# A delta-rule attention block and a gated feed-forward block on one core: two more units fetched in blocks, one more pair's first layer by 20 block products, and a new order of all work

## The chip, the core and the metric

The kernel runs on one core of one Trainium2 chip. The metric is device time in microseconds. Before the change it was measured in three runs: 637.15, 640.19 and 640.47 us, with a median of 640.19.

A core has five engines that run beside each other and wait for one another through semaphores. TensorE (PE in the profile, with PEld for the loads of its stationary operand) does matrix products. VectorE (DVE), ScalarE (ACT) and GpSimd (POOL) do elementwise work. SyncE (SP) starts transfers; ScalarE and GpSimd can start them too. Each engine takes its instructions in the order in which they were written, so an instruction that waits holds up all that stand behind it on its engine.

## What is computed

```python
# 4 batches, 8 heads, 768 positions, head size 48
k_n = k / (norm(k) + 1e-06)
state = zeros(4, 8, 48, 48)
for t in range(768):
    y[:, :, t] = q[:, :, t] @ state
    v_old = state^T @ k_n[:, :, t]
    state += beta[:, :, t] * outer(k_n[:, :, t], v[:, :, t] - v_old)
x = y as (3072 tokens, 384)
h = x @ w_in            # 384 -> 2048
g = h * cos(h)
out = g @ w_out         # 2048 -> 384
```

## The kernel before

**Units and pairs.** The 768 positions are cut into 24 units of 32. The four batches fill the 128 partitions. Within a unit the recurrence is written as a triangular system: the products of all keys with each other (the gram matrix) give a 32 x 32 triangle for each batch and head, whose inverse is needed to get the unit's updates. Only the 48 x 48 states pass from unit to unit. Two units make a pair of 256 tokens; there are 12 pairs, and the feed-forward block runs pair by pair.

**One unit**, in the names of its tasks (function `unit`, L1492): load k, q and v; norms of k (`square`, `sum`, `norms`, `scale`); `turn`, which puts k and q with the head dimension on partitions; `gram` (L673), whose results VectorE scales and masks into g (`gram_keys`, L694) and tt (`gram_queries`, L813); the inverse of the triangle; then the serial part: `state` (L928, products with the state), `right` (L945), `solve` (L1000, or L958, L958, L994 in three steps for units 2 and 3), `solve_out` (L1012), `update` (L1025), `update_out` (L1033), `within` (L1043 or L1055), `within_out` (L1068), `features` (L1076) and `features_out` (L1084). Unit n+1's `state` needs unit n's `update_out`.

**Inverses, three ways.** Units 0 and 1 invert by doubling: six rounds of small products on TensorE (`double`, L757), each followed by copies, additions and 32 x 32 transposes on ScalarE and VectorE. All others go pair by pair, the 16 matrices of a partition group laid out so that GpSimd can eliminate column by column: g is written to DRAM (`gram_put`), read back (`gram_get` into gb), inverted by pairs of operations (`inv`, L877 and L884), written to DRAM (`put`) and read back as zt (`get`). gb, z and zt have one buffer each. Pair 1 (units 2 and 3) does this at half size.

**Two ways of turning.** For units below `PLAIN_TURNS` (8) k and q are loaded whole, TensorE turns them (L640, eight transposes a unit) and ScalarE copies the result out (L650). From `PLAIN_TURNS` on, k and q are fetched a second time in blocks of 32 columns (`load_blocks`, L415, eight transfers a unit), which VectorE turns by 32 x 32 transposes (`turn_blocks`, L660, four a unit); k is loaded in eight parts instead of four and g stored in three instead of one, with half of the heads on swapped partitions ("home"), and `weigh` and beta follow that.

**The feed-forward block.** The first layer is computed two ways. For pairs in `ONES` (0 and 1) it is plain: eight groups (`hidden`, L1097) of twelve products. For the others (`gated`) 20 block products (`layer`, L1271) of sums of x blocks (`x_sum`, L1186) with sums of w_in blocks (`in_sums`, L1233, 22 of them once, twelve in place in w_in, so that they must follow the last plain group) replace the 24 block products of a plain first layer, and the results are put together by copies on ScalarE (L1283, L1285) and additions on VectorE (L1288). Then come x cos x by ScalarE and VectorE (`turns` L1134, `rest` L1141, `cos` L1150, `gate` L1153) and the second layer: plain for pair 0 (`out`, L1295), by seven products of half size (L1353, with sums of gates L1369, sums of w_out L1382 and collecting L1405) for the rest. The weights come as 64-bit words and are narrowed to 32 bits on chip, 28 pieces in the tasks `weights`, `split`, `shift` and `add`; the pieces' buffers are those of the gates.

**The order of the work.** Nothing schedules at run time. Every piece of work is a task with the tasks it depends on and the buffers it makes and uses (`add`); the arguments for cost, transfer time and due time are those of a planner that isn't part of the kernel. `Order.LINE` lists all tasks by number in the order in which they are written out, `Order.OTHER` the tasks that go to the second choice of two engines or queues:

```python
def queue(*key):
    return nc.scalar if key in Order.OTHER else nc.sync
...
        for key in line:
            emit, deps, makes, uses = self.tasks[key]
            assert deps <= done, key
```

Which buffer a task gets follows from the order too. At the end every instruction is pinned behind the one before it on its engine, and transfers behind each other across SP's and ScalarE's queues.

**Unread products.** `keep_warm` (L493) multiplies a constant tile into the output bank, and nobody reads it. `WARM_FIRST` (5) are written at the start; `WARMS` (56) are tasks, each of which does something only as long as no output product has been written (31 of the 56).

Of the kernel before, what the change touches and what calls it, by code (L numbers as in the profile page):

```python
# [59 lines left out]
class Order:  # L60

    OTHER = {
        ('gram_put', 2), ('q', 3), ('gram_get', 1), ('inv', 1, 0), ('put', 1), ('gram_put',
        4), ('gram_put', 5), ('v', 7), ('v', 8), ('v', 9), ('blocks', 11, 1), ('gram_put',
        11), ('put', 5), ('v', 13), ('put', 6), ('gram_put', 15), ('gram_get', 7), ('get',
        15), ('v', 16), ('blocks', 16, 0), ('blocks', 16, 1), ('gram_put', 16), ('blocks',
        18, 1), ('k', 19), ('blocks', 19, 0), ('gram_get', 9), ('get', 19), ('gram_put',
        20), ('v', 21), ('gram_put', 21), ('put', 10), ('gram_put', 22), ('v', 23),
        ('gram_put', 23), ('gram_get', 11), ('right', 4, 4), ('left', 1, 1, 0), ('left', 1,
        3, 0), ('left', 1, 3, 1), ('store', 1, 0), ('x_sum', 2, 'd'), ('x_sum', 2, 'n'),  # L70
        ('x_sum', 2, 'm'), ('x_sum', 2, 'e'), ('x_sum', 2, 'k'), ('x_sum', 2, 'g'),
        ('x_sum', 2, 'i'), ('x_sum', 2, 'l'), ('x_sum', 2, 'f'), ('x_sum', 2, 'b0'),
        ('left', 2, 4, 1), ('left', 2, 3, 1), ('x_sum', 3, 'd'), ('x_sum', 3, 'n'),
        ('x_sum', 3, 'm'), ('x_sum', 3, 'e'), ('x_sum', 3, 'k'), ('x_sum', 3, 'g'),
        ('x_sum', 3, 'i'), ('x_sum', 3, 'l'), ('x_sum', 3, 'h'), ('x_sum', 3, 'b0'),
        ('left', 3, 4, 1), ('left', 3, 3, 1), ('x_sum', 4, 'd'), ('x_sum', 4, 'm'),
        ('x_sum', 4, 'g'), ('x_sum', 4, 'i'), ('left', 4, 3, 0), ('left', 4, 3, 1),
        ('store', 4, 0), ('x_sum', 5, 'd'), ('x_sum', 5, 'e'), ('x_sum', 5, 'l'), ('x_sum',
        5, 'h'), ('x_sum', 5, 'b0'), ('left', 5, 2, 0), ('left', 5, 4, 1), ('left', 5, 3,
        0), ('left', 5, 3, 1), ('store', 5, 0), ('x_sum', 6, 'd'), ('x_sum', 6, 'g'),  # L80
        ('x_sum', 6, 'l'), ('x_sum', 6, 'f'), ('x_sum', 6, 'b0'), ('left', 6, 1, 0),
        ('left', 6, 4, 0), ('store', 6, 1), ('x_sum', 7, 'd'), ('x_sum', 7, 'm'), ('x_sum',
        7, 'g'), ('x_sum', 7, 'i'), ('x_sum', 7, 'f'), ('x_sum', 7, 'h'), ('x_sum', 7,
        'b0'), ('left', 7, 4, 0), ('left', 7, 4, 1), ('left', 7, 3, 1), ('x_sum', 8, 'd'),
        ('x_sum', 8, 'm'), ('x_sum', 8, 'e'), ('x_sum', 8, 'k'), ('x_sum', 8, 'g'),
        ('x_sum', 8, 'l'), ('left', 8, 3, 0), ('store', 8, 0), ('store', 8, 1), ('x_sum', 9,
        'd'), ('x_sum', 9, 'm'), ('x_sum', 9, 'e'), ('x_sum', 9, 'k'), ('x_sum', 9, 'i'),
        ('x_sum', 9, 'l'), ('x_sum', 9, 'b0'), ('left', 9, 1, 0), ('left', 9, 2, 0),
        ('left', 9, 1, 1), ('left', 9, 3, 0), ('store', 9, 0), ('x_sum', 10, 'k'), ('x_sum',
        10, 'i'), ('x_sum', 10, 'l'), ('x_sum', 10, 'h'), ('x_sum', 10, 'b0'), ('left', 10,  # L90
        1, 0), ('left', 10, 1, 1), ('left', 10, 4, 1), ('left', 10, 3, 0), ('left', 10, 3,
        1), ('store', 10, 0), ('x_sum', 11, 'd'), ('x_sum', 11, 'e'), ('x_sum', 11, 'k'),
        ('x_sum', 11, 'g'), ('x_sum', 11, 'f'), ('left', 11, 1, 0), ('left', 11, 2, 0),
        ('left', 11, 1, 1), ('left', 11, 3, 0), ('left', 11, 3, 1), ('store', 11, 1),
        ('store_right', 11), ('weights', 5), ('weights', 7), ('weights', 15), ('weights',
        16), ('weights', 18), ('weights', 20), ('weights', 22), ('weights', 23), ('weights',
        25), ('weights', 27)
    }

    WARM_FIRST, WARMS = 5, 56  # L100
    LINE = """
# [138 lines left out]
def kernel(  # L240
# [1197 lines left out]
    ONES, PLAIN = range(2), range(1)  # L1438
# [508 lines left out]
```

## Time and profile before

The profile is of one execution. Its span, from the first to the last instruction, is 636.6 us; 24189 instructions are in it. The time of a run has what lies around the span in it, and the three runs shown lie 0.5 to 3.9 us above this span.

| engine | busy, us | share of the span |
|---|---|---|
| TensorE products | 619.2 | 97% |
| TensorE weight loads | 576.2 | 90% |
| VectorE | 495.1 | 78% |
| GpSimd | 435.8 | 68% |
| ScalarE | 297.7 | 47% |

How to read it: an engine's busy time is the time in which an instruction of it was under way, a wait for a semaphore not counted. A plain float32 product stands as two records (two passes), a transpose as one. In rows of the timeline the columns are start, duration, engine, line, operation, result<-operands, size, count, and in brackets the idle time before it with what ended it. In rows of the stretches, the busy time of each engine is followed by the count of instructions; then come the clock that was granted to TensorE (1.00 is full), the share of the transfer engines and their rate.

Three waits, from the groups of the page: GpSimd's inversions (L877) stood idle 21.2 us for gb from DRAM, ScalarE's L1150 waited 42.6 us for VectorE, and VectorE's L1405 28.0 us for TensorE's second layer.

### The profile page before, as it was taken

How to read it: one execution, taken by the hardware profiler on the slowest of the kernel's cores; microseconds unless marked ns; L12 is line 12 of the kernel's file. 1: busy time of each engine (PE TensorE's matmuls, PEld its weight loads, DVE VectorE, ACT ScalarE, POOL GpSimd, SP SyncE). 2: the span in 40 equal slices, each digit the busy share in tenths (PEclk: the TensorE clock that was granted, in tenths of full speed). 3: DMA queues.
4: the chain of work that ended last, by engine and by line, in shares of the span. 5: the costliest groups of instructions: out<-in, count | busy, mean ns of one | idle time of the engine just before them, and what ended most of it. 6: DMA issues, size and time to landing. Idle time of an engine off the chain costs nothing.

```text
span 636.6 us, 24189 instructions
## 1 busy us (share of the span) xinstructions
PE 619.2 (97%) x10176; PEld 576.2 (90%) x10176; DVE 495.1 (78%) x1030; ACT 297.7 (47%) x528; POOL 435.8 (68%) x780
## 2 busy tenths in 40 slices
PE   5999989999999999999999999999999999999997
PEld 4877877987899999999999999999999999999997
DVE  5776656779998999887898888888888776566682
ACT  3457556562423444643642644733643553545440
POOL 5247788678788788887789888886884883112241
PEclk8899999999999999999999999999999999999999
DMA  8978656563651555435435344333304102000001
GB/s 173 221 171 213 121 155 146 93 118 60 116 68 22 94 90 99 60 67 104 61 70 98 56 73 90 58 57 67 74 3 81 44 1 43 19 2 26 1 25 26
DMA packets 209381, 50.37 MB, mean 79 GB/s; under 512 B 200920, under 2 KB 204280, under 8 KB 209272
## 3 DMA queue, kind: packets, MB, share of 16 engines
q1 hardware_dynamic: 161896, 35.03, 29.3%
q10 hardware_dynamic: 47072, 13.25, 10.0%
q8 instruction: 80, 1.31, 0.9%
q0 software_dynamic: 304, 0.54, 0.4%
q14 instruction: 29, 0.24, 0.1%
HBM read 38.55 MB, written 10.22 MB: 77 GB/s over the span
## 4 chain that ended last, share of the span: by engine, by line
PE 90%; DVE 3%; DMA 3%; ACT 1%; issue 1%; POOL 0%; SPq 0%; ACTq 0%; DVEq 0%
PE p_out L1353 29%; PE p_h L1271 27%; PE p_h L1097 6%; PE p_kq L928 4%; PE p_out L1295 3%; PE p_s L1025 3%; PE p_g L673 3%; PE p_h L757 3%; PE p_kq L1055 3%; PE p_u L1000 3%; PE p_out L493 2%; PE p_h L1353 2%; PE p_z L1076 1%; DMA kp<-in_k_dram 1%; PE p_t L640 1%
## 5 line engine op out<-in xcount | busy, mean ns | idle before, releaser
L877 POOL TENSOR_TENSOR part<-z,gb 128x126 f32<-128x126 f32 (+23 forms) x321 | 144.6, 451 | 46.7 <-DMA gb<-g_dr 21.2
L884 POOL TENSOR_TENSOR z<-z,part 128x126 f32<-128x126 f32 (+23 forms) x321 | 145.5, 453 | 25.1
L1353 PE MATMUL p_out<-w_out,g_ffn 128*128 128x192 f32 x672 | 121.9, 328 | 0.3 <-DVE o L1405 0.2
L1353 PEld LDWEIGHTS p_out<-w_out,g_ffn 128*128 128x128 f32 x672 | 107.7, 190 | 1.7 <-DVE o L1405 0.7
L1150 ACT ACTIVATE turns<-turns,halfpi 128x512 f32<-128x512 f32 x96 | 68.0, 719 | 55.7 <-DVE turns L1141 42.6
L1353 PE MATMUL p_out<-w_sum,g_ffn 128*128 128x192 f32 x496 | 89.7, 329 | 0.2 <-DVE o L1405 0.2
L1271 PE MATMUL p_h<-x_sum,w_in 128*128 128x128 f32 x640 | 84.0, 277 | 0.0
L1134 ACT ACTIVATE turns<-g_ffn,quarter_turn 128x512 int32<-128x512 f32 x70 | 49.8, 719 | 66.4 <-DVE g_ffn L1288 31.3
L1353 PEld LDWEIGHTS p_out<-w_sum,g_ffn 128*128 128x128 f32 x496 | 79.6, 190 | 1.2 <-issue 0.4
L1271 PEld LDWEIGHTS p_h<-x_sum,w_in 128*128 128x128 f32 x640 | 78.8, 192 | 1.1
L1288 DVE TENSOR_TENSOR g_ffn<-g_ffn,p_h 128x512 f32<-128x512 f32 x80 | 54.3, 681 | 17.3 <-PE p_h L1271 16.4
L1141 DVE SCALAR_TENSOR_TENSOR turns<-g_ffn,turns 128x512 f32<-128x512 f32 x70 | 55.3, 796 | 13.1 <-ACT turns L1134 13.0
L1068 ACT COPY y<-p_kq 32x384 f32<-32x384 f32 x96 | 45.2, 470 | 30.4 <-PE p_kq L1055 22.5
L1153 DVE TENSOR_TENSOR g_ffn<-turns,g_ffn 128x512 f32<-128x512 f32 x70 | 51.5, 745 | 3.8 <-ACT turns L1150 3.7
L1271 PE MATMUL p_h<-x_sum,in_sum 128*128 128x128 f32 x400 | 52.9, 277 | 0.0
L572 POOL TENSOR_TENSOR knrm<-ksum,halves 128x16 f32<-128x16 f32 (+1 forms) x14 | 36.4, 2602 | 23.9 <-DMA qp<-in_q_dram 12.6
L1271 PEld LDWEIGHTS p_h<-x_sum,in_sum 128*128 128x128 f32 x400 | 49.7, 192 | 0.8
L1405 DVE SCALAR_TENSOR_TENSOR o<-p_out,o 128x192 f32<-128x192 f32 x74 | 25.1, 351 | 28.4 <-PE p_out L1353 28.0
L1097 PE MATMUL p_h<-x_ffn,w_in 128*128 128x128 f32 x384 | 45.8, 277 | 0.0
L1097 PEld LDWEIGHTS p_h<-x_ffn,w_in 128*128 128x128 f32 x384 | 44.1, 192 | 1.2
L1271 PE MATMUL p_h<-x_ffn,w_in 128*128 128x128 f32 x320 | 42.4, 277 | 0.0
L1369 POOL TENSOR_TENSOR g_ffn<-g_ffn,g_ffn 128x512 f32<-128x512 f32 x18 | 25.8, 1442 | 22.5 <-PE p_out L1353 18.7
(168 smaller groups left out, 1071.3 us busy)
## 6 DMA issues: line engine op xcount, KB each, us to landing
g_ffn<-in_moe_w_in_dram SPq DMA_DIRECT2D x10, 512.0 KB
gb<-g_dr SPq DMA_DIRECT2D x14, 256.0 KB
vp<-in_v_dram SPq DMA_DIRECT2D x68, 48.0 KB
g_ffn<-in_moe_w_out_dram SPq DMA_DIRECT2D x8, 384.0 KB
g_ffn<-in_moe_w_out_dram ACTq DMA_DIRECT2D x8, 384.0 KB
kp<-in_k_dram SPq DMA_DIRECT2D x120, 24.0 KB
out_dram<-o SPq DMA_DIRECT2D x14, 192.0 KB
zt<-z_dr SPq DMA_DIRECT2D x72, 32.0 KB
```

What stands on the lines that cost most here:

```text
L572: nc.gpsimd.tensor_tensor(out=scales[m][2][:, part], in0=sums[m, part.start][:, 0:n], in1=halves[:, 0:n], op=ALU.pow,)
L877: eng.tensor_tensor(out=part, in0=z[:, 0:rows, j, None].to_broadcast(shape), in1=a[:, j, None, j + 1 :].to_broadcast(shape), op=ALU.mult,)
L884: eng.tensor_tensor(out=behind, in0=behind, in1=part, op=ALU.subtract)
L1068: nc.scalar.copy(by_parity(y[quarter(b)]), p_kq[quarter(b ^ 1), :, b % 2])
L1097: nc.tensor.matmul(p_h[:, i], w_in[:, t, (4 * k + i) * 128 : (4 * k + i + 1) * 128], xts[p][:, t, unit * 128 : (unit + 1) * 128], start=(i ...
L1134: nc.scalar.activation(turns[p, f], hidden_of(p, f), AF.Identity, bias=quarter_turn, scale=TURN)
L1141: nc.vector.scalar_tensor_tensor(out=r, in0=hidden_of(p, f), scalar=TURN, in1=t, op0=ALU.mult, op1=ALU.subtract,)
L1150: nc.scalar.activation(r, r, AF.Sin, bias=halfpi, scale=2.0 * math.pi)
L1153: nc.vector.tensor_tensor(out=place(p, f), in0=step_of(rests.pop((p, f)), f), in1=step_of(hidden_of(p, f), f), op=ALU.mult,)
L1271: nc.tensor.matmul(p_h[:, e], in_block(*w)[:, e], x_of(p, b), start=new and e == 0, stop=True, skip_group_check=True,)
L1288: nc.vector.tensor_tensor(out=part_of(p, to), in0=part_of(p, one), in1=part_of(p, two), op=op)
L1353: nc.tensor.matmul(p_o, left(p, part, a)[:, e % 4], right(e, b), start=(e == 0), stop=(e == FT // 2 - 1), skip_group_check=True,)
```

## The change

`PLAIN_TURNS` goes from 8 to 6, `ONES` from two pairs to one, `WARMS` from 56 to 5, one dependency of the sums of w_in blocks is loosened, and `OTHER` and `LINE` are new throughout (2187 tasks instead of 2196). Nothing else differs. The two tables are cut here to their first lines.

```diff
     OTHER = {
-        ('gram_put', 2), ('q', 3), ('gram_get', 1), ('inv', 1, 0), ('put', 1), ('gram_put',
-        4), ('gram_put', 5), ('v', 7), ('v', 8), ('v', 9), ('blocks', 11, 1), ('gram_put',
...
+        ('k', 2), ('gram_put', 2), ('inv', 1, 0), ('blocks', 6, 0), ('blocks', 8, 1), ('v', 10),
+        ('blocks', 10, 0), ('gram_put', 10), ('blocks', 11, 1), ('gram_get', 5),
...
-    WARM_FIRST, WARMS = 5, 56
+    WARM_FIRST, WARMS = 5, 5
     LINE = """
-0 1 66 2 70 2084 3 71 4 8 9 72 122 67 68 5 2085 123 69 127 73 128 124 65 75 125 80 76 77 2088 178 78
...
+0 1 2075 15 16 17 2 127 19 20 21 3 4 5 18 71 2076 72 128 22 24 76 73 77 74 25 8 29 30 31 26 23 130
...
-    PLAIN_TURNS = 8
+    PLAIN_TURNS = 6
...
-    ONES, PLAIN = range(2), range(1)
+    ONES, PLAIN = range(1), range(1)
...
-                deps += [("solve", n) for n in range(4)] + [("within", n) for n in range(2)]
+                deps += [("solve", n) for n in (range(4) if to in (S6, S7) else range(1))]
```

What the new order does in the first 100 us, as far as the prediction speaks of it: all six doubling rounds of unit 0 stand ahead of unit 1's second round, and the first solve follows. The loads of k and q of unit 2 stand ahead of the second piece of weights. The first plain group of pair 0 stands behind unit 1's solve, update and gram of unit 5 instead of ahead of that solve; the next three stand around unit 2's state. The eleven sums of x blocks of pair 1 are on GpSimd. The second-layer products of pair 0 are spread among pair 1's block products, and eight additions of weight pieces stand between the columns of inversion 2 on GpSimd, where there were four.

More of the change, by code (lines that the diff above doesn't have):

```diff
@@ L62 @@
     OTHER = {
-        ('gram_put', 2), ('q', 3), ('gram_get', 1), ('inv', 1, 0), ('put', 1), ('gram_put',
-        4), ('gram_put', 5), ('v', 7), ('v', 8), ('v', 9), ('blocks', 11, 1), ('gram_put',
[L65 to L80, printed above, removed]
@@ L87 @@
-        'd'), ('x_sum', 9, 'm'), ('x_sum', 9, 'e'), ('x_sum', 9, 'k'), ('x_sum', 9, 'i'),
+        ('k', 2), ('gram_put', 2), ('inv', 1, 0), ('blocks', 6, 0), ('blocks', 8, 1), ('v', 10),
+        ('blocks', 10, 0), ('gram_put', 10), ('blocks', 11, 1), ('gram_get', 5),
+        ('blocks', 14, 0), ('blocks', 14, 1), ('gram_get', 7), ('v', 16), ('get', 16),
+        ('gram_put', 17), ('get', 17), ('gram_put', 18), ('blocks', 19, 0), ('put', 9),
+        ('get', 20), ('v', 21), ('gram_put', 22), ('put', 11), ('right', 4, 4),
@@ new lines @@
+        ('left', 1, 1, 0), ('left', 1, 3, 0), ('left', 1, 3, 1), ('store', 1, 1),
+        ('x_sum', 2, 'd'), ('x_sum', 2, 'n'), ('x_sum', 2, 'm'), ('x_sum', 2, 'e'),
+        ('x_sum', 2, 'k'), ('x_sum', 2, 'g'), ('x_sum', 2, 'i'), ('x_sum', 2, 'l'),
+        ('x_sum', 2, 'f'), ('x_sum', 2, 'b0'), ('left', 2, 4, 1), ('left', 2, 3, 1),
+        ('x_sum', 3, 'd'), ('x_sum', 3, 'n'), ('x_sum', 3, 'm'), ('x_sum', 3, 'e'),
+        ('x_sum', 3, 'k'), ('x_sum', 3, 'g'), ('x_sum', 3, 'i'), ('x_sum', 3, 'l'),
@@ new lines @@
+        ('x_sum', 3, 'h'), ('x_sum', 3, 'b0'), ('left', 3, 4, 1), ('left', 3, 3, 1),
+        ('store', 3, 1), ('x_sum', 4, 'd'), ('x_sum', 4, 'm'), ('x_sum', 4, 'g'),
+        ('x_sum', 4, 'i'), ('left', 4, 3, 0), ('left', 4, 3, 1), ('store', 4, 0),
+        ('x_sum', 5, 'd'), ('x_sum', 5, 'e'), ('x_sum', 5, 'l'), ('x_sum', 5, 'h'),
+        ('x_sum', 5, 'b0'), ('left', 5, 2, 0), ('left', 5, 4, 1), ('left', 5, 3, 0),
+        ('left', 5, 3, 1), ('store', 5, 0), ('x_sum', 6, 'd'), ('x_sum', 6, 'g'),
@@ L88 @@
+        ('x_sum', 9, 'm'), ('x_sum', 9, 'e'), ('x_sum', 9, 'k'), ('x_sum', 9, 'i'),
         ('x_sum', 9, 'l'), ('x_sum', 9, 'b0'), ('left', 9, 1, 0), ('left', 9, 2, 0),
[L89 to L92, printed above, removed]
+        ('left', 9, 1, 1), ('left', 9, 3, 0), ('x_sum', 10, 'k'), ('x_sum', 10, 'i'),
@@ L93 @@
+        ('x_sum', 10, 'l'), ('x_sum', 10, 'h'), ('x_sum', 10, 'b0'), ('left', 10, 1, 0),
+        ('left', 10, 1, 1), ('left', 10, 4, 1), ('left', 10, 3, 0), ('left', 10, 3, 1),
+        ('store', 10, 0), ('x_sum', 11, 'd'), ('x_sum', 11, 'e'), ('x_sum', 11, 'k'),
         ('x_sum', 11, 'g'), ('x_sum', 11, 'f'), ('left', 11, 1, 0), ('left', 11, 2, 0),
         ('left', 11, 1, 1), ('left', 11, 3, 0), ('left', 11, 3, 1), ('store', 11, 1),
-        ('store_right', 11), ('weights', 5), ('weights', 7), ('weights', 15), ('weights',
```

15 lines of the change are left out of this document (8 added, 7 removed), and 197 rows, old and new, of the table LINE.

## The prediction

> **What bounds the kernel now.** I read the page's busy shares first, then its chain, then a table of stretches, then the timeline of TensorE alone.
>
> ```profile
> PE 619.2 (97%) x10176; PEld 576.2 (90%) x10176; DVE 495.1 (78%) x1030; ACT 297.7 (47%) x528; POOL 435.8 (68%) x780
> PE 90%; DVE 3%; DMA 3%; ACT 1%; issue 1%; POOL 0%; SPq 0%; ACTq 0%; DVEq 0%
> ```
>
> TensorE is busy 97% of the span and holds 90% of the chain. So two things count: how much TensorE has to do, and how long it stands or does useless work. The stretches (span, busy us of TensorE, weight loads, VectorE, ScalarE and GpSimd, granted clock, DMA share, GB/s) tell where:
>
> ```profile
> 4.00:11.00 7.00, 4.41 (x86) 3.39 (x85) 1.75 (x4) 3.38 (x6) 2.79 (x4) 1.00 1.17 209
> 11.00:21.00 10.00, 7.05 (x124) 5.71 (x123) 9.35 (x28) 4.35 (x9) 2.96 (x6) 0.50 0.84 199
> 102.00:112.00 10.00, 10.00 (x157) 8.63 (x154) 8.49 (x17) 6.55 (x12) 8.59 (x19) 1.00 0.74 170
> 140.00:200.00 60.00, 60.00 (x1002) 52.00 (x1000) 55.34 (x112) 21.70 (x41) 49.87 (x94) 1.00 0.44 71
> 200.00:300.00 100.00, 99.38 (x1801) 94.71 (x1799) 86.27 (x178) 47.87 (x82) 85.88 (x161) 1.00 0.45 78
> ```
>
> From 102 us on TensorE has no gaps to speak of. Before that it has, and the timeline shows that even its busy time there is partly filler:
>
> ```profile
> 47.09 1.14 PE L1000 MATMUL p_u<-vp,in_sum 64*64 64x48 f32 x32 [0.73 <-ACT kq_t L650]
> 63.00 1.13 PE L493 MATMUL p_out<-o 128*128 128x256 f32 x4
> 64.06 1.13 PE L1000 MATMUL p_u<-rhs,w_sum 64*64 64x48 f32 x32
> 73.57 1.15 PE L928 MATMUL p_kq<-st,kq_t 48*64 48x48 f32 x64
> ```
>
> L493 is a product that nobody reads. Between the first turn (6.1 us) and 102 us I count from this timeline 18.1 us of such products (31 of them), 8.9 us of gaps, 3.0 us lost to the half clock before 21.5 us, and some 7 us of tasks longer than their kind: **37 us lost**. All of the remaining 500 us lose another 6. In the first 100 us the bound is therefore not TensorE but the serial chain of units 0 to 3, run mostly by VectorE.
>
> **Part 1: products removed.** Pair 1's first layer was 8 groups of 24 records (12 products, each in two records), 2.73 us from group to group (L1097): 21.8 us. It becomes 20 groups of 8 records, 0.90 us each (L1271, 0.89 back to back): 18.0. Units 6 and 7 lose their turns on TensorE (L640, 0.93 us each): 1.9. So TensorE gets **5.7 us** less, and after 102 us it is the bound, so this goes to the end in full if nothing else becomes late. Everything else that TensorE does stays the same: the other nine first layers, all second layers and all units.
>
> What other engines get: VectorE 10 additions (L1288, 0.68), 8 block turns (L660, 0.41), 7 gatings in SBUF that are 0.18 longer (0.796 and 0.745 against 0.683 and 0.681), and unit pair 3's scaling by homes, 0.7: 12 us. ScalarE nine copies (L1283, 0.58) less four (L650, 0.59): +3. GpSimd eleven x sums, 0.56 each (L1186): 6. The queues of SP and ScalarE get 20 more DMA starts (16 for blocks in place of 8 for q, 8 more for k, 4 more for g). ScalarE (47% busy) and the queues hide theirs; the DMA share between 81 and 102 us is 0.41 to 0.59, so the blocks of units 6 and 7 should land in time. If not, VectorE stands at their turn with unit 3's right side behind it. I price that at 0, bounds 0 to 3 (one load of 1.6 to 3 us). VectorE and GpSimd are part 3.
>
> **Part 2: the early chain.** The built order puts unit 0's doubling ahead of unit 1's. In the order before, its six rounds start at 14.9, 19.0, 26.0, 33.5, 38.7 and 43.8 us, with unit 1's rounds and weight shifts between them, and the first solve is at 47.1. VectorE's instructions ahead of that solve sum to 35.6 us by their rows; in the new order to 29.9. VectorE starts at 8.7 us and overlaps neighbours, so that 35.6 us cost 31.0 of busy time (factor 0.87). The floor is 8.7 + 29.9 x 0.87 = 34.7 us instead of 39.7. Up to unit 2's state (L928, 73.57) both orders have the same 54.4 us of VectorE ahead and the same TensorE work but for fillers and one turn, so the floor is 8.7 + 47.3 = 56.0 in both; the kernel now stands 17.6 us above it. In the new order less of this is left: a hidden group of 2.9 us no longer stands ahead of the second solve, and unit 1's rounds fill the waits of unit 0's chain, as L493 did. Going through the new order with the rows I come to 37 us for the first solve, 54 for the second and 66 to 67 for unit 2's state: a gain of 7. The bounds are 0 (it waits as now) and 17.6 (no wait).
>
> Against it stands the clock. The row of 4 to 11 us has TensorE busy 4.41 of 7 us, and the next ten us are granted at 0.50. The new order drops 26 of the 31 fillers, so TensorE will be half idle up to about 55 us. The trace shows what half clock costs: a round of 16 products takes 1.97 us instead of 1.09. I take 1 us off the gain, so **6 us**. The Trainium skill ("TensorE: Matmul & The Clock Gate", the clock gate of Part 1, and its list of why this matters) says that a window of some 3.4 us without enough work halves the clock and that a busy one restores it. The trace agrees as far as it goes: one half-clock stretch of about 10 us, right after a thin one. By that rule alone the fillers were worth keeping and this term would be nearer to 0; it is the third rival.
>
> **Part 3: later.** Here I expect something to be given back. The loop through GpSimd runs gram(2m+1), keys, DRAM, inversion, DRAM, solve(2m). Its shortest passage in the timeline: keys end 205.2, inversion starts 215.5, lasts 34.2, ends 249.8, its last reading DMA has started by 254.7 and lands by about 256.7 (2.0 us, as the chain has for a g_dr transfer). With the 0.8 us of gram, that is 10.3 + 34.2 + 7 + 0.8 = 52 us. The work that TensorE has between that gram and that solve was 55 to 62 us; in the new order it is 51 to 53 for m = 2 to 6, and 56 to 64 after. So the cover is gone five times. GpSimd itself, from the end of inversion 2 to that of inversion 6, has four inversions of 33.5 and 33.5 us of other work (167.5) while TensorE has 163.2 from the fourth unit's solve to the twelfth's: 4.3 us short. VectorE from unit 2's solve to unit 11's has 166.8 us of its own time against 169.9 of TensorE (98%); before it was 159.9 against 185.4. In 140:200 it is busy 92% and TensorE doesn't wait, so 98% is over what is shown to be free; 166.8 / 0.94 is 177.4, or 7.5 us of waiting, and these waits and GpSimd's are the same microseconds. Before, the stretch lost 7.7. From unit 2's solve to the end the kernel loses 10.7 us now; I take 12.2, **1.5 us more** (bounds -5 and +14).
>
> **Sum.** -5.7 - 6 + 1.5 = -10.2 us. The profiled span of 636.6 becomes 626.4. The runs shown are 637.15, 640.19 and 640.47; the span lies 3.6 below their median, and I keep that distance: **630.0 us**. A measurement of this kernel tells about 0.5% from no change, which is 3.2 us: faster means under 637.0.
>
> **Rivals.**
>
> A. Nothing is given back: the 7 us of part 2 in full, and after unit 2's solve only the 6 us of the last 500 lost, not 10.7: -5.7 - 7 - 4.7 = -17.4, **623**. For it: GpSimd's loop has slack of 3 to 4 us in each pair. Against: the 98%.
>
> B. GpSimd's loop takes the gain. Ten inversions now start 44.4 us apart. If they keep that pace, inversion 6 ends 179.7 us after inversion 2, which would end at 108, and unit 12's solve comes at 108 + 179.7 + 7 = 294.7, against 306.1 now, 11.4 earlier; but TensorE's work behind that solve is 333.3 us by the rows in the new order and 324.3 in the old, 9.0 more. So the end is 2.4 earlier: **637.8**, no change. For it: L877 waits 21.2 us for gb. Against: part of the 44.4 us is waiting for TensorE.
>
> C. The clock stays at half until the first hidden group, for want of fillers. TensorE has 29.7 us of work up to there by its rows, 59.4 at half clock. With 6.1 ahead and 12 of waits the group starts at 77.5 instead of the 59.1 that I came to; 18.4 later, so -5.7 - 7 + 1.5 + 18.4 = +7.2: **647**, slower. It decides once the half clock costs over 11 us. For it: the 0.50 above. Against: at half clock TensorE's tasks fill twice the time, and after 21 us, with TensorE busy again, the clock stayed full through idle tenths.
>
> The block products of pair 1 are in the built order (220 groups instead of 200), so that the change doesn't do what it says is left out.
>
> **Chances.** Forecast 0.50 (625 to 635), A 0.15, B 0.20, C 0.15. Faster: forecast, A and a quarter of B, 0.70; same 0.14; slower 0.16. The range leaves out a quarter of A and nearly all of C: 620 to 643.
>
> **What would show it.** L1097 should have 192 records instead of 384, L640 48 instead of 64, and L493 20 instead of 72. Part 2: first solve (L1000) near 38 us, third L928 near 67.5; 73 or later refutes it. Clock: a row below 0.8 between 21 and 55 us speaks for C. Part 3: TensorE idle between 100 and 290 us of 6 to 10 us, ended by zt's DMA at L1000 or by VectorE's gates; under 3 speaks for A, over 14 for B. I am wrong if a chain that I did not walk (weights into w_in, ScalarE's FIFO) ends last in the first 100 us.

## The result, and the profile after

The changed kernel takes **669.47 us** (median of 4 runs, 668.47 to 671.61), the kernel before 639.91 in the same rounds (4 runs, 637.15 to 640.47). The ratio is 1.0479, 95% interval 1.045 to 1.0509: **slower by 4.8%**. Forecast were 630.0 and, as the range, 620 to 643. The profiled span grew from 636.6 to 667.7 us, the mean granted clock fell from 0.991 to 0.972.

The page of the kernel after, busy shares and chain of waits (lines of code lie two lower than before: L1097 is L1095, L1000 is L998):

```profile
PE 615.0 (92%) x10076; PEld 571.8 (86%) x10076; DVE 511.5 (77%) x1051; ACT 301.5 (45%) x533; POOL 438.3 (66%) x791
PE 20%; DVE 3%; DMA 2%; issue 0%; ACT 0%; SPq 0%; POOL 0%; DVEq 0%
```

No engine's share has risen; TensorE's fell from 97% to 92%. The chain adds up to 25% only, so it covers no more than a quarter of the span and says nothing of where the rest went. The stretches do (columns as before):

```profile
4.00:11.00 7.00, 3.06 (x13) 1.90 (x11) 1.70 (x3) 1.90 (x3) 2.48 (x4) 0.93 1.15 198
11.00:21.00 10.00, 7.44 (x173) 6.01 (x174) 7.44 (x24) 5.68 (x12) 1.98 (x3) 0.54 0.80 149
41.00:51.00 10.00, 6.31 (x58) 5.65 (x62) 8.91 (x20) 4.78 (x9) 4.98 (x5) 0.66 0.55 121
102.00:112.00 10.00, 6.19 (x108) 3.74 (x109) 6.85 (x14) 3.15 (x6) 5.28 (x9) 0.83 0.73 142
140.00:200.00 60.00, 53.57 (x931) 45.39 (x930) 50.59 (x107) 24.73 (x43) 46.94 (x94) 0.94 0.41 68
200.00:300.00 100.00, 93.69 (x1705) 88.55 (x1705) 82.10 (x171) 45.57 (x79) 81.25 (x155) 0.97 0.43 71
```

Behind 102 us, where TensorE had no gaps, it now has them in every row. The row to look at is the last. In these 100 us *every* engine is less busy than before: TensorE 93.69 instead of 99.38, VectorE 82.10 instead of 86.27, GpSimd 81.25 instead of 85.88, ScalarE 45.57 instead of 47.87, and the transfers have a share of 0.43 instead of 0.45. If the load of one of them had become the bound, its number would have risen.

For the balance I use one measure, an estimate: **lost** is TensorE's time since its first turn (6.13 us) less its work by the usual durations of its tasks. Before, it lost 43.0 us over 583.9 of work and ended at 633.0; after, 79.6 over 578.3, ending at 664.1. The 31.1 us between are -5.6 of work and +36.6 of loss (rounded), and nearly all of the loss lies behind 100 us. There TensorE loses 45 us instead of 6: it stands for 28.8 of the 564.1 us from 100 us to its end, and the other 16 are lost in tasks longer than their kind. What it stood for, behind 100 us (total, times, longest, in us):

```profile
PE p_u L998 <- DMA zt<-z_dr: 6.8, 4, 3.3
PE p_h L1269 <- ACT p_h L1281: 6.8, 3, 5.4
PE p_u L992 <- DVE g_ffn L976: 3.1, 1, 3.1
PE p_h L1269 <- POOL x_sum L1184: 3.0, 2, 2.0
PE p_out L1351 <- DVE o L1403: 3.0, 3, 1.7
PE p_h L1269 <- DVE x_ffn L1184: 1.4, 1, 1.4
```

In the kernel before, the same view has 4 waits of 1.6 us in all; here it has 20 of 28.6 us: VectorE 11.6, ScalarE 7.2, transfers 6.8, GpSimd 3.0. So the waits are few at a time and come from all sides.

The clock adds to them. Four stretches behind 100 us are granted at exactly half, each right behind one in which TensorE stood; before, there was none between 21.5 us and the last product. Two of them, each with the 3.4 us ahead of it:

```profile
153.40:156.80 3.40, 1.46 (x96) 1.20 (x88) 0.00 (x0) 0.00 (x0) 2.93 (x7) 0.99 0.43 82
156.80:163.60 6.80, 3.33 (x11) 2.72 (x12) 2.81 (x4) 3.82 (x7) 5.71 (x14) 0.50 0.36 60
221.60:225.00 3.40, 0.95 (x8) 0.66 (x7) 1.26 (x5) 2.25 (x4) 2.08 (x7) 1.00 0.30 47
225.00:231.80 6.80, 5.99 (x46) 5.93 (x46) 1.80 (x3) 1.56 (x2) 5.63 (x16) 0.50 0.33 58
```

All four together are 20.4 us long, with TensorE busy for 15.6 of them. Half of that, 7.8 us, is an estimate of what half clock costs there. The waits are the larger part, and they come first; some 9 us of longer tasks are left that neither accounts for.

### The profile page after: what moved, and what is told of

The parts are those of the page before. It is cut to its first block, busy times and chain, and to the rows that moved or that the text cites. A ratio compares the mean times of both kernels' runs of the same rounds, so it can differ in the third digit from the quotient of the medians.

```text
span 667.7 us, 24016 instructions
## 1 busy us (share of the span) xinstructions
PE 615.0 (92%) x10076; PEld 571.8 (86%) x10076; DVE 511.5 (77%) x1051; ACT 301.5 (45%) x533; POOL 438.3 (66%) x791
## 5 line engine op out<-in xcount | busy, mean ns | idle before, releaser
L875 POOL TENSOR_TENSOR part<-z,gb 128x126 f32<-128x126 f32 (+23 forms) x321 | 141.8, 442 | 38.1 <-DMA gb<-g_dr 12.0
L882 POOL TENSOR_TENSOR z<-z,part 128x126 f32<-128x126 f32 (+23 forms) x321 | 144.2, 449 | 25.2
L1269 PE MATMUL p_h<-x_sum,w_in 128*128 128x128 f32 x704 | 93.0, 280 | 6.7 <-ACT p_h L1281 6.3
L1269 PEld LDWEIGHTS p_h<-x_sum,w_in 128*128 128x128 f32 x704 | 86.3, 193 | 9.4 <-ACT p_h L1281 7.1
L1132 ACT ACTIVATE turns<-g_ffn,quarter_turn 128x512 int32<-128x512 f32 x77 | 54.8, 719 | 66.6 <-DVE g_ffn L1286 28.8
L1286 DVE TENSOR_TENSOR g_ffn<-g_ffn,p_h 128x512 f32<-128x512 f32 x88 | 59.4, 679 | 17.1 <-PE p_h L1269 16.1
L1139 DVE SCALAR_TENSOR_TENSOR turns<-g_ffn,turns 128x512 f32<-128x512 f32 x77 | 57.8, 756 | 15.3 <-ACT turns L1132 15.2
L1151 DVE TENSOR_TENSOR g_ffn<-turns,g_ffn 128x512 f32<-128x512 f32 x77 | 57.2, 746 | 11.4 <-ACT turns L1148 11.4
L1269 PE MATMUL p_h<-x_sum,in_sum 128*128 128x128 f32 x440 | 60.3, 283 | 3.5 <-POOL x_sum L1184 3.0
L1269 PEld LDWEIGHTS p_h<-x_sum,in_sum 128*128 128x128 f32 x440 | 54.6, 194 | 5.6 <-POOL x_sum L1184 3.2
L1066 ACT COPY y<-p_kq 32x384 f32<-32x384 f32 x96 | 45.1, 470 | 24.3 <-PE p_kq L1053 20.4
L570 POOL TENSOR_TENSOR knrm<-ksum,halves 128x16 f32<-128x16 f32 (+1 forms) x14 | 36.6, 2611 | 22.9 <-DVE ksum L558 22.9
L1403 DVE SCALAR_TENSOR_TENSOR o<-p_out,o 128x192 f32<-128x192 f32 x74 | 25.1, 351 | 31.1 <-PE p_out L1351 28.3
L1269 PE MATMUL p_h<-x_ffn,w_in 128*128 128x128 f32 x352 | 47.1, 277 | 0.0
L1367 POOL TENSOR_TENSOR g_ffn<-g_ffn 128x512 f32<-128x512 f32 x15 | 21.2, 1417 | 36.9 <-DVE g_ffn L1151 34.1
```

Of the source, the lines that this page charges most:

```text
L570: nc.gpsimd.tensor_tensor(out=scales[m][2][:, part], in0=sums[m, part.start][:, 0:n], in1=halves[:, 0:n], op=ALU.pow,)
L875: eng.tensor_tensor(out=part, in0=z[:, 0:rows, j, None].to_broadcast(shape), in1=a[:, j, None, j + 1 :].to_broadcast(shape), op=ALU.mult,)
L882: eng.tensor_tensor(out=behind, in0=behind, in1=part, op=ALU.subtract)
L1066: nc.scalar.copy(by_parity(y[quarter(b)]), p_kq[quarter(b ^ 1), :, b % 2])
L1132: nc.scalar.activation(turns[p, f], hidden_of(p, f), AF.Identity, bias=quarter_turn, scale=TURN)
L1139: nc.vector.scalar_tensor_tensor(out=r, in0=hidden_of(p, f), scalar=TURN, in1=t, op0=ALU.mult, op1=ALU.subtract,)
```

## The experiments

Three theories at first. **ORDER**: the new order of all tasks makes the engines wait for each other, whatever the work. **WORK**: the added work of VectorE, GpSimd and the queues does it. **CLOCK**: the fillers had kept the clock up. Once ORDER was ahead, three pairs of forms of it: transfers late in SP's queue (**LANDING**) or VectorE and GpSimd behind (**LAG**), a list of single misplaced instructions (**LOCAL**) or no slack anywhere (**DIFFUSE**); and the early (**EARLY**) or the later (**LATE**) part of the order.

The table has each kernel's time and where TensorE lost, by its profiled run. Times without an interval below are of one run each, beside before's median of 638.5 to 639.9 on the same chip. "Old" and "new" say which of the two orders the tasks stand in up to 85 us and behind.

| kernel | work | order to 85, behind | time, us | lost to 100 | 100 to 200 | behind 200 |
|---|---|---|---|---|---|---|
| before | old | old, old | 639.91 | 36.8 | 1.1 | 5.1 |
| after | new | new, new | 669.47 | 34.4 | 19.6 | 25.6 |
| e1 | old, 5 fillers | old, old | 638.07 | 35.3 | 1.2 | 6.9 |
| e2 | old, 5 fillers | new, new | 671.69 | 36.6 | 16.6 | 23.0 |
| e3 | new | new; old behind 205 | 648.82 | 35.0 | 17.3 | 6.7 |
| e4 | old, late blocks | old, old | 645.90 | 39.6 | 6.2 | 6.1 |
| e5 | new, 17 fillers | new, new | 670.96 | 38.8 | 18.7 | 23.8 |
| e6 | new, fewer transfers | new, new | 653.88 | 36.5 | 12.0 | 15.5 |
| e7 | old, fewer transfers | old, old | 637.51 | 36.3 | 1.0 | 4.7 |
| e8 | new, no gate sums | new, new | 650.66 | 34.1 | 15.0 | 11.4 |
| e9 | new | re-made | 665.35 | 36.4 | 18.9 | 20.8 |
| e10 | old, 5 fillers | re-made | 656.23 | 37.4 | 2.4 | 20.0 |
| e11 | old, no gate sums | old, old | 638.16 | 37.1 | 1.7 | 3.8 |
| e12 | new, both left out | new, new | 651.31 | 36.7 | 13.8 | 11.0 |
| e13 | new | new, two tasks moved | 666.01 | 37.7 | 13.6 | 25.2 |
| e14 | old, 5 fillers | new, old | 648.67 | 42.4 | 4.6 | 6.1 |
| e15 | old, 5 fillers | old, new | 667.89 | 32.5 | 13.0 | 26.6 |

### One part of the change at a time: e1, e2, e4, e5

**e1**, the kernel before with the fillers cut:

```diff
-    WARM_FIRST, WARMS = 5, 56
+    WARM_FIRST, WARMS = 5, 5
```

> The kernel before with 5 fillers among the tasks in place of 56, all else in its order; 26 fewer unread products run. Three theories are tried in this series. ORDER: the new fixed order has no room left in it, so each late landing and each lag of VectorE or GpSimd becomes a wait of TensorE, and the added work itself is harmless. WORK: VectorE, GpSimd and the queues have more to do (12, 6 us and some 20 more starts), and TensorE waits for them in any order. CLOCK: the fillers kept the clock up, and without them TensorE runs at half clock. CLOCK expects 650 or more here and rows of half clock between 21 and 60 us. ORDER and WORK expect no loss: 26 x 0.55 us of products leave the first 100 us, of which what stood in idle time gains nothing, so 626 to 640, and no half clock behind 25 us.

Measured: 638.07 (10 runs) against 639.41 (13 runs), ratio 0.9971 (0.9946 to 0.9995), granted clock 0.992. CLOCK's 650 did not come, but some of its half clock did: 3.4 us at 46.0 and 3.4 at 63.1 us, where the kernel before has none and ORDER and WORK had expected none. The first stretch is shorter for it, 3.4 us at 15.3 instead of 10.2 at 11.1, so there are 10.2 us of half clock in both. Fillers shift where the clock drops, and it costs nothing on balance: taking out most of their products gave 0.3%. Nearly all of them stood where TensorE had to wait anyway: its idle time from 6.1 to 100 us rises from 9.7 to 21.0. It is the only one of these kernels with all the work that is faster than the one before, by less than the 0.5% that the prediction set as its bound.

**e2**, the changed kernel with the old work put back and its new order kept:

```diff
-    PLAIN_TURNS = 6
+    PLAIN_TURNS = 8
-    ONES, PLAIN = range(1), range(1)
+    ONES, PLAIN = range(2), range(1)
```

> The work of before (two plain pairs, units 6 and 7 turned by TensorE) in the new order, with 5 fillers: eight plain groups stand where pair 1's 20 groups stood, and the two turns where VectorE's turns were fetched for. ORDER expects it as slow as the changed kernel: its 669 plus up to 5.7 us of products that are back, 660 to 675. WORK expects that it comes back to the time of before: 645 or less. CLOCK expects what the changed kernel shows, half clock in some six stretches, and 660 or more too; it is told from ORDER by the first run.

LINE has the old tasks where the new ones stood, and OTHER loses the one entry of a transfer that isn't there.

Measured: 671.69. With none of the added work the loss is all there: ORDER, and WORK is off the table as the main cause. CLOCK expected the same here; e1 speaks against it.

**e4**, the kernel before with the blocks of units 6 and 7 alone, in the places where their loads of q stood:

```diff
-    PLAIN_TURNS = 8
+    PLAIN_TURNS = 6
```

> The kernel before with units 6 and 7 fetched in blocks and turned by VectorE, the blocks' transfers where those of q stood; order and fillers as before. ORDER expects within 4 us of the kernel before: 1.9 us of turns less on TensorE, VectorE 4 us more. WORK expects 5 us or more on top, since blocks land late and VectorE stands at their turn: 645 or more. CLOCK expects no change.

Measured: 645.90, ratio 1.0099 (1.0081 to 1.0118), as WORK expected (645 or more) and not as ORDER did (within 4 us). So the added work is not harmless in the old order: this part costs 6.5 us by itself, although it takes 1.9 off TensorE. In the view of VectorE's waits between 60 and 140 us the turning of blocks has the two longest single waits; before it had none:

```profile
DVE kq_t L660 <- DMA g_dr<-g: 3.9, 1, 3.9
DVE kq_t L660 <- PE p_kq L928: 3.1, 1, 3.1
```

The changed kernel has such a wait too, in VectorE's timeline, put down to the blocks' own transfer:

```profile
101.75 1.42 DVE L658 STREAM_TRANSPOSE kq_t<-qp 128x256 f32<-128x256 f32 x4 [3.81 <-DMA qp<-in_k_dram]
```

The block transfers of unit 7's keys are started at 96.24 us; on SP's queue they stand behind eight readings of an inverse that were started at 90.90. VectorE waits 3.81 us for them, with a step of unit 3's solution behind it (L976), and TensorE stands 3.1 for that.

**e5**, the changed kernel with 12 more fillers in places where TensorE stood:

```diff
-    WARM_FIRST, WARMS = 5, 5
+    WARM_FIRST, WARMS = 5, 17
```

> The changed kernel with 12 more unread products, put where TensorE stood for 0.8 us or more between 8 and 104 us (7 of them in the 4.3 us at 40.4, ahead of the stretch of half clock from 44.1 to 50.9). CLOCK expects that this stretch goes and that what it cost, 3 us, stays won to the end, with more behind it: 666 or less. ORDER expects full clock there too, but the next wait takes the 3 us back: 667 to 671.

Measured: 670.96, ratio 1.0485 (1.0419 to 1.0551), clock 0.979. The 6.8 us of half clock at 44.1 have become 3.4 at 40.8, and the end is no earlier. As the main cause CLOCK has fallen; fillers behind 104 us were not tried.

### Which part of the order: e3, e14, e15

**e3**, the changed kernel with the tasks that started behind 205 us in the order of before:

```diff
     LINE = """
...
-... 297 1001 441 987 985 988 340 1006 930 298 299 1002 1003 388 ...
+... 297 1001 987 340 341 342 343 344 796 921 930 419 329 932 ...
```

> The changed kernel, its order kept for all that starts before 205 us; all later tasks stand in the order that they have in the kernel before. In the changed kernel TensorE's time beyond its work grows from 54 to 80 us behind 200 us, in the kernel before by some 5. ORDER expects that most of this goes: 20 us less than the changed kernel, 645 to 653. WORK expects little, as all the work is there: 663 or more. CLOCK expects no change in the first 205 us and little behind them: 663 or more.

Measured: 648.82, as ORDER expected. All the new work is in it, and behind 200 us it loses 6.7 us instead of 25.6. Its row answers to the last one above:

```profile
200.00:300.00 100.00, 98.26 (x1761) 93.29 (x1760) 84.72 (x177) 47.70 (x84) 82.64 (x156) 1.00 0.43 74
```

Every engine is busier than in the changed kernel, since TensorE hardly waits. **e14** and **e15** do the same at 85 us, crosswise and with the old work and 5 fillers: e14 has the new order up to there and the old behind, e15 the old up to there and the new behind. In the edits of LINE, e14 first differs from e2 at the 219th task, e15 from e1 at the 290th. In all three, as in e2, the entries of OTHER go with the tasks, so "order" means two things: the place in line, and whether SP's or ScalarE's queue starts a transfer.

```diff
     LINE = """
...
-... 176 2072 249 2085 2082 2078 122 205 123 223 13 124 ...
+... 176 2072 2085 2082 2078 122 205 123 223 13 124 741 ...
```

```diff
     LINE = """
...
-... 2102 749 150 2109 2103 755 152 273 151 257 258 2113 ...
+... 2102 749 2109 2103 273 2113 229 230 7 881 755 757 ...
```

> All work of the kernel before (two pairs plain, whole loads up to unit 7) with 5 fillers, in the new order for every task that starts before 85 us in the changed kernel's trace, and in the order of before for all the rest. Beside it stand the same work wholly in the old order (638.1) and wholly in the new (671.7). If what is lost after 100 us comes from the order written behind 85 us (LATE): TensorE keeps what it has at 85 us and loses 10 us at most behind it, so 632 to 646. If the new early order hands a backlog on (loads, VectorE's and GpSimd's queues) that the rest can't take up (EARLY): 655 to 675.

> The other half: the same work and 5 fillers, in the order of before for every task that starts before 85 us in that kernel's trace, and in the new order for all the rest. LATE: the loss is there, 660 to 675 (the wholly new order has 671.7). EARLY: it is not, 638 to 648. Both halves slow (each between 648 and 660) would say that the two parts of the order fit each other and that neither half carries the loss alone.

Measured: 667.89 for e15, as LATE expected. e14 has 648.67, which misses LATE's range by 2.7 us. Where it loses tells them apart all the same: behind 100 us 10.7 us, beside 8.1 in e1, while e15 loses 39.6 there and e2 39.6. What e14 has on top is at the seam, where the two orders were joined: 42.4 lost up to 100 us, and this row, with the clock at half for most of it:

```profile
81.00:102.00 21.00, 16.07 (x445) 14.34 (x437) 8.19 (x18) 10.67 (x21) 11.77 (x27) 0.66 0.57 135
```

So the early order hands hardly any backlog on. The loss is in the order written behind 85 us. Whether it lies in the places or in the queues no run tells for certain. The changed kernel starts 573 transfers on SP's queue, the kernel before 525; but e6, below, starts 481 and is still 14 us slower than the kernel before, so the load of that queue is not all of it. How it looks there, in e15's timeline of TensorE around 150 us:

```profile
149.10 1.14 PE L995 MATMUL p_u<-rhs,zt 64*64 64x48 f32 x32
150.16 2.85 PE L1290 MATMUL p_out<-w_out,g_ffn 128*128 128x384 f32 x8
158.54 1.56 PE L1020 MATMUL p_s<-u,kp 64*64 64x96 f32 x32 [5.53 <-DVE u L1007]
```

and in VectorE's, beside it:

```profile
148.31 2.40 DVE L1228 TENSOR_TENSOR w_in<-w_in 128x512 f32<-128x512 f32 x3 [1.59 <-PE p_h L1092]
...
154.74 1.52 DVE L1228 TENSOR_TENSOR w_in<-w_in,in_sum 128x512 f32<-128x512 f32 x2
156.19 0.68 DVE L1136 SCALAR_TENSOR_TENSOR turns<-p_h,turns 128x512 f32<-128x512 f32 x1
156.79 0.68 DVE L1228 TENSOR_TENSOR w_in<-w_in,in_sum 128x512 f32<-128x512 f32 x1
157.38 1.01 DVE L1007 TENSOR_TENSOR u<-p_u,bz 128x384 f32<-128x384 f32 x2
```

The solution is there at 150.2 us, but VectorE has idled for 1.59 us up to 148.31 and then has an unbroken run of sums of w_in ahead of the two operations that TensorE is waiting for. They come at 157.38. VectorE had just been idle; it has the urgent work behind sums that were written ahead of it.

### Which relief helps: e6, e7, e8, e11, e12

Two reliefs, each in both orders. e6 and e7 leave out the block transfers of units 10 and later, so that these turn the keys and queries of older units; e8 and e11 leave out the 88 sums of gates for the second layer (55 on VectorE, 33 on GpSimd), so that its products read what the buffers hold; e12 leaves out both.

```diff
     def load_blocks(n, a, eng=nc.sync):
+        if n >= 10:
+            return
...
     def left_sum(p, x, s):
+        return
```

> The changed kernel without the block transfers of units 10 and later (112 of its 681 starts on the queues of SP and ScalarE); these units turn the blocks of earlier ones, so their keys and queries are not computed from the input. Two forms of ORDER: LANDING says that TensorE's waits begin at transfers that start late behind others in SP's queue (0.5 us each, in runs of up to 48) or land late; it expects 10 us or more less than the changed kernel: 659 or less, and the waits for zt (6.8 us) under 2. LAG says that they begin at VectorE and GpSimd, which the new order lets fall behind; it expects 665 or more.

> The kernel before without the same block transfers (units 10 and later turn old blocks). LANDING and LAG both expect little here, since TensorE waits for hardly anything behind 100 us in this order: 633 to 640. If it gains as much as the new order does, the transfers cost the same in any order and LANDING falls as the cause of the difference.

> The changed kernel without the 88 sums of gates for the second layers (55 on VectorE, 33 on GpSimd; the products read the gates themselves, so the second layers of pairs 1 to 11 are not the reference's). That takes some 40 us from VectorE and 45 from GpSimd, against 12 and 6 that the change put on them. WORK, and LAG as far as it is a matter of load, expects 10 us or more less than the changed kernel: 659 or less. ORDER, with the waits starting at transfers and at single instructions in the wrong place, expects 664 or more.

> The kernel before, without the 88 sums of gates that the second layers' left operands need (55 on VectorE, 33 on GpSimd), so that these operands hold what was there. It is the fourth corner of a square: the same relief took 18.8 us off the changed kernel, and fewer transfers took 15.6 off the changed kernel and 2.3 off the one before. If the new order has no slack, so that any relief pays there and none pays in the old one: 635 to 639 (at most 4 off). If the sums themselves are what bounds either kernel (LOAD): 621 to 628, as much off as in the new order.

> The changed kernel without the 88 sums of gates and without the block transfers of units 10 and later (their turned keys and queries are those of older units). Taken one by one they gave 18.8 and 15.6 us. LANDING and LAG as two separate causes: the gains add up, 669.5 - 34 = 635, between 631 and 640. One shared cause that either relief cures (a chain that passes through both): 648 to 652, hardly better than the better of the two. In both cases the first 200 us keep most of their loss (49 us lost on TensorE at 200 us in each of the two), so under 630 is expected by neither.

| | old order | new order |
|---|---|---|
| nothing left out | 639.9 | 669.5 |
| fewer transfers | 637.5 (-2.4) | 653.9 (-15.6) |
| no gate sums | 638.2 (-1.7; -0.6 to before on its chip) | 650.7 (-18.8) |
| both | not run | 651.3 (-18.2) |

These are single runs. The four runs of the changed kernel lie within 3.1 us, those of e5 within 8.6 and those of the kernel before within 3.3, so the gains in the new order are clear but can't be ranked, and those in the old order can't be told from none.

e6 looked like LANDING by itself (659 or less), and its wait for zt had shrunk, if not to under 2:

```profile
PE p_u L1000 <- DMA zt<-z_dr: 2.3, 3, 1.0
```

Then e8 came out as WORK and LAG had expected (659 or less) and not as ORDER had, with its waits starting at transfers and single instructions (664 or more): taking work off VectorE and GpSimd helps as much, with all transfers in place, and its wait for zt is down to 3.7 us too. e11 shows that the sums are no bound by their load, which would have given 621 to 628. And e12 shows that the two reliefs don't add up. So neither is *the* cause. In the new order each of these two, on different engines and queues, takes off 16 to 19 us and both together no more; in the old order either takes off 2.4 at most. That is what a schedule without slack would look like beside one with slack. But e12's second theory, one shared cause such as a chain that passes through both, expected 648 to 652 and fits as well; no run parts the two. What neither relief cures is the stretch from 100 to 200 us, where 12 to 15 us stay lost.

### Single instructions, or everywhere: e13, e9, e10

**e13** moves only what TensorE was seen to wait behind longest. One is the turning of unit 7's keys above. The other is the squares of unit 5's keys, for which ScalarE stood with a copy behind it that TensorE needed:

```profile
158.28 0.84 ACT L553 ACTIVATE g_ffn<-kp 128x768 f32<-128x768 f32 x1 [6.38 <-DMA g_dr<-g]
160.27 2.08 PE L1269 MATMUL p_h<-x_sum,w_in 128*128 128x128 f32 x8 [5.42 <-ACT p_h L1281]
```

```diff
     LINE = """
-... 768 2160 277 181 2167 ... 793 186 187 327 ...
+... 768 2160 181 2167 ... 793 186 277 187 327 ...
...
-... 875 360 829 240 877 241 787 242 894 244 361 895 896 876 879 ...
+... 875 829 240 877 241 787 242 894 244 895 896 876 360 361 879 ...
```

> The changed kernel with two things moved in its order and nothing else: the turning of unit 7's keys (turn_out 7) from ahead of unit 3's last gates to behind unit 3's solution, and the squares and sums of unit 5's keys behind the sums of two more block products. In the changed kernel VectorE stands 3.8 us at the one, ScalarE 6.4 at the other, TensorE behind them 3.1 and 5.4, each time with a stretch of half clock behind it. If the loss is a list of single misplaced instructions (LOCAL): both waits of TensorE and both half-clock stretches go and stay gone at the end, 8 to 12 us, 657 to 662. If the order has no slack anywhere behind (DIFFUSE): the two waits go, but what is gained at 165 us is mostly waited for again by 340 us, 664 to 672.

Measured: 666.01, ratio 1.0407 (1.0358 to 1.0456). The wait of 5.4 us is gone, that of 3.1 has become 0.7, and of the 20.4 us of half clock behind 100 us 7 are left. The time is DIFFUSE's figure; LOCAL expected 8 to 12 us less. But it didn't come about as DIFFUSE said, by waiting again up to 340 us for what was gained: by the table e13 loses 6.0 us less than the changed kernel from 100 to 200 us and 0.4 less behind, and it had lost 3.3 more up to 100, where the two programs are alike up to 85. A wait of 2.6 us for a sum of x blocks is new; the 6.1 us for zt were 6.8 before. So the two moves are worth some 6 us behind 100 us in this pair of profiles, short of LOCAL's 8, and stay won; the intervals of e13 and the changed kernel overlap. Between LOCAL and DIFFUSE it decides nothing.

**e9** and **e10** have orders re-made by moving single tasks for as long as the instruction durations recorded in six of these runs promised a gain, e9 with the new work and e10 with the old and 5 fillers. Against the changed kernel and e1, LINE (and OTHER with it) is other from the 17th task on:

```diff
     LINE = """
...
-... 18 71 2076 72 128 22 24 76 73 77 74 25 8 29 ...
+... 18 71 72 22 24 76 73 2076 74 25 8 29 130 77 ...
```

```diff
     LINE = """
...
-... 17 5 2034 72 18 76 22 77 73 14 24 74 ...
+... 17 5 72 18 76 22 77 73 14 24 74 25 ...
```

> All the work of the changed kernel (20 block products for pair 1, blocks for units 6 and 7, 5 fillers) in an order re-made from that of the run with the late order of before: single tasks moved a few places on their engine, so that the order bears the durations, starts and landings that six runs of this series measured, and not only the usual one of each kind. ORDER expects it faster than the kernel before: 626 to 636. WORK expects that no order helps by more than the late order of before did: 645 or more.

> The work of before with 5 fillers, its order re-made in the same way from that of the run with few fillers. ORDER expects 624 to 634: the order before had room for improvement too. The difference to the run with the new work is what the two moved parts are worth once both orders are made with the same care: the prediction's sum says 5.7 us in favour of the new work; WORK says that the old work is the faster by 10 or more.

Measured: 665.35 (ratio 1.0413, 1.0387 to 1.0438) and 656.23 (1.0265, 1.0239 to 1.0291). Both miss, by 29 and 22 us, and on the same side as the change itself. They are also 16.5 and 18.2 us slower than the kernels whose orders they were made from, e3 and e1. An order fitted to a list of durations promised what the chip did not give. Between the two, the old work is the faster by 9.1 us, where the prediction's sum had the new work ahead by 5.7 and WORK the old by 10 or more; with e4 that suggests, without showing it, that the added work has a price of its own. How far the chip's times move by themselves is seen where the programs are alike: up to 85 us the changed kernel, e8, e12 and e13 have the same instructions in the same order, and unit 2's solution starts at 83.3, 82.2, 86.7 and 86.7 us. In e12 and e13 the clock is at half from 9 to 23 us, at 40 and from 47 to 53, in the changed kernel from 10 to 20 and from 44 to 51, and in e8 from 9 to 22 and not again up to 85.

**What stays open.** That the loss comes with the order written behind 85 us is shown. What in it costs the time was seen at three places (VectorE's sums ahead of u, the blocks of unit 7, the squares of unit 5), not for all 36 us; places and queues were not parted, and that the order has no slack is argued from the reliefs. The block products of pair 1 were not tried alone in the old order, so whether their 3.8 us of work saved would be kept there isn't known. Why e9 and e10 fall short by so much is argued, not shown.

## Why the prediction was wrong

**Part 1, products removed: right.** TensorE's work by rows fell from 583.9 to 578.3 us, 5.6 as against 5.7. The records are as said, here the plain first layers (half of 384) and the 20 fillers:

```profile
L1095 PE MATMUL p_h<-x_ffn,w_in x192: 269/275/377, 65.5 to 100.6; 128*128 128x128 f32 x192
L491 PE MATMUL p_out<-o x20: 379/634/796, 1.3 to 61.6; 128*128 128x256 f32 x20
```

The late blocks, priced at 0 with bounds of 0 to 3, were mis-sized. VectorE stands 3.81 us in the changed kernel, and this part alone costs 6.5 in the old order (e4).

**Part 2, the early chain: its first step right, the rest not.** TensorE's timeline has:

```profile
39.27 1.08 PE L998 MATMUL p_u<-vp,in_sum 64*64 64x48 f32 x32
44.69 1.97 PE L755 MATMUL p_h<-w_sum 64*64 64x128 f32 x16 [4.34 <-DVE w_sum L771]
60.02 1.33 PE L998 MATMUL p_u<-rhs,w_sum 64*64 64x48 f32 x32 [0.21 <-DVE w_sum L775]
72.43 1.15 PE L926 MATMUL p_kq<-st,kq_t 48*64 48x48 f32 x64
```

The first solve came at 39.27, near 38 as said, 7.8 earlier than before. The second came at 60.02 instead of 54: unit 1's rounds, now behind it, find VectorE late by 4.34 us, and then run at half clock (1.97 for 16 products, the price that the prediction had). Unit 2's state is at 72.43 instead of 66 to 67.5, 1.1 us ahead of before and just short of the 73 that was to refute the step. By unit 2's solution the loss is 32.6, beside 32.5. So the gain of 6 was 0. The Trainium skill ("TensorE: Matmul & The Clock Gate", section "What's actually happening") gives a window of 3413 ns that runs free of the program. The trace agrees: half clock comes in stretches of 3.4, 6.8 or 10.2 us, at 44.1 to 50.9 here, right behind the wait.

**Part 3, later: the failed step.** "I take 12.2, 1.5 us more (bounds -5 and +14)" measured 47.0 from unit 2's solution to the end, 36.6 more than the 10.4 of before. The step added up what VectorE and GpSimd have to do over 167 us and compared it with TensorE's work: 98% full, so 7.5 us of waiting. (The 1.5 doesn't follow from that: 7.5 in the place of the 7.7 lost before is 0.2 less, not 1.5 more.) That sum can't see what happened. In the 190 us from 100 to 290 the changed kernel has

```profile
100.00:290.00 190.00, 171.48 (x3179) 152.18 (x3178) 160.58 (x324) 84.57 (x150) 151.91 (x282) 0.95 0.47 82
```

VectorE is busy 85% of it and GpSimd 80%, less than before (164.91 and 155.94 us), and TensorE stands 18.5 us. Nobody was full. What the sum leaves out is when each operand comes. Behind 100 us TensorE waits 20 times for another engine or a transfer, for 28.6 us in all; before it was 3 times, for 1.1 (the fourth wait above was for neither). With the same work it is 7 times and 3.5 us with the old order behind 85 us (e14), and 20 times and 22.3 us with the new (e15).

**The sum** was -5.7 - 6 + 1.5. Measured by TensorE's end in the two profiles it is -5.6 + 0.1 + 36.6 = +31.1; the medians differ by 29.6.

**The rivals.** A (nothing given back) fell with part 3. B held GpSimd's loop for the bound: unit 12's solution would come at 294.7; it came at 317.2. Waits for zt are there, but they are 6.8 of 28.6 us, GpSimd's own wait for gb between 100 and 500 us fell from 21.2 to 12.0, and leaving out sums of gates (e8) paid no less than leaving out transfers (e6). C's half clock came, and with it the sign on record, a row below 0.8 between 21 and 55 us (0.66 from 41 to 51); but it came for 6.8 us at 44.1 and not up to the first hidden group, and at unit 2's solution nothing was lost on balance. Slower was given 0.16, nearly all of it to C's mechanism. What came true wasn't among the rivals: that the new order, as an order, costs some 30 us behind 85 us, with the old work as with the new.

The sign to look for was on record, TensorE idle between 100 and 290 us "over 14 for B". It is 18.5, and yet not B, since the sign asked how long and not behind whom: zt's part in that stretch is 3.3 us.

## What to carry to other kernels

When a change re-orders a program of in-order engines, sums of work by engine give only a floor: here TensorE stood 18.5 of 190 us with no engine fuller than before. Price the order by walking it: for each product of the bound engine, what stands ahead of its operand on the producing engine and queue. To tell order from work, put the old work into the new order (e2) and graft half of one order onto the other (e14, e15). And try reliefs that have nothing to do with each other: if each pays, both together pay no more and neither pays in the old order, then no one engine's load is the cause.

## What the runs showed of the hardware

The granted clock takes two values, 0.50 and 1.00, and changes on a grid of about 3.4 us: 3.4 us stretches at 105.6 and 122.6 us, 6.8 at 44.1, 156.8 and 225.0, and 10.2 at 10.0. In the 3.4 us ahead of the four behind 100 us TensorE was busy for 0.81, 1.99, 1.46 and 0.95 us. Yet 3.4 us with 1.62 busy, from 334.2, were followed by full clock, so the busy share alone, as the profile has it, doesn't tell. TensorE's wait of 3.1 us that ended at 104.7 is followed by 3.4 us at half speed, and a round of 16 products takes 1.97 us at half clock instead of 1.09. Twelve more fillers in the new order shortened one stretch from 6.8 to 3.4 us (e5), and 26 fewer in the old order brought two of 3.4 us and shortened another by 6.8 (e1). The medians moved by 0.2% and 0.3%.

A start of a transfer takes SP's queue about half a microsecond, so a run of starts is itself a delay. In SP's timeline of the changed kernel the reading of inverse 13 stands behind such a run, and zt, with one buffer, is late for its solution:

```profile
316.00 1.80 SPq L394 DMA_DIRECT2D kp<-in_k_dram  x4
317.85 3.12 SPq L394 DMA_DIRECT2D vp<-in_v_dram  x4
321.02 2.46 SPq L413 DMA_DIRECT2D qp<-in_q_dram  x4
...
328.61 4.93 SPq L394 DMA_DIRECT2D kp<-in_k_dram  x8
333.64 0.59 SPq L1418 DMA_DIRECT2D out_dram<-o  x1
334.27 2.00 SPq L906 DMA_DIRECT2D zt<-z_dr  x4
```

TensorE takes up the solution at 339.08, having stood 3.26 us for it. The starts shown are 0.45 us (1.80 for 4) to 0.78 (3.12 for 4) long on average.
